# Ten dk stores dealt anew over the DMA engines (nine without engine 4, with strips by SyncE) in the backward pass of decode attention

## The chip, the cores and the metric

One core of one Trainium2 chip. The metric is the device time of one execution in microseconds (us); most executions of one kernel here agree within 0.3%, and differences of a few tenths of a per cent are settled only by several runs of both kernels on the same chip. "Engine 0 to 15" means the 16 DMA engines of the core; PE, DVE, ACT, GpSimd (POOL) and SyncE (SP) are named as such.

## The reference

```python
def _fwd_reference(q, k, v):            # q: (2, 32, 1, 128), k and v: (2, 32, 8192, 128), bfloat16
    scale = q.shape[-1] ** -0.5
    p = softmax(einsum("bhqd,bhkd->bhqk", q, k) * scale)
    return einsum("bhqk,bhkd->bhqd", p, v)

def reference(q, k, v, grad_out):
    out, vjp = jax.vjp(_fwd_reference, q, k, v)
    return out, *vjp(grad_out)          # out, dq, dk, dv
```

One query per head, 64 heads. For each head 2 MB of k and 2 MB of v are read, and 2 MB of dk and 2 MB of dv are written; everything else is small. So the kernel is a stream of 128 loads and 128 stores of 2 MB.

## The kernel before

k and v of a head live in two of twelve tiles of 128 partitions x 64 x 128 bfloat16 (one row of 16 KB per partition). dk and dv are written over k and v in the same tile, the tile is stored, and the load of a head six further on refills it. SyncE issues the loads, GpSimd the stores; each engine issues in program order.

```python
load_eng = nc.sync
store_eng = nc.gpsimd
pin = tc.keep_in_program_order
NTILE = 12
FIRST = 6                       # rows of q loaded by GpSimd at the start: puts its cursor at 6
SPREAD = range(4, 60, 7)        # eight heads whose dk store is split into 126 + 2 rows

def by_rows(eng, dst, src, rows):
    p = 0
    for m in rows:
        pin(eng.dma_start(out=dst[p : p + m], in_=src[p : p + m], max_dma_last_dim=NT * D))
        p += m

def outer(i, w, c, ends):       # writes dv (w = 1) or dk (w = 0) over the tile; at its end:
    ...
        if w == 0 and i in SPREAD:
            by_rows(store_eng, dst, h.tile[w], (P - 2, 2))
        else:
            eng = load_eng if len(ends) > 1 else store_eng     # len(ends) > 1: the last head only
            pin(eng.dma_start(out=dst[:, b0:b1, :], in_=h.tile[w][:, b0:b1, :]))

# in the main loop, O1 and O0 are where dv and dk of a head begin, NCH = 4 steps each
if (i := at(O1 + NCH)) is not None and i + AHEAD < BH:
    load(i + AHEAD, 0)          # refills dv's tile
if (i := at(O0 + NCH)) is not None and i + AHEAD < BH:
    load(i + AHEAD, 1)          # refills dk's tile
if x := within(O1): outer(x[0], 1, x[1], ...)
if x := within(O0): outer(x[0], 0, x[1], ...)
```

## Time and profile before

| what | where it is read | value |
|---|---|---|
| time | 3 runs | 1279.65 us median (1277.72 to 1282.9); the profiled run, slower than all of these, 1285.99 |
| span | first line of the page | 1284.2 us |
| busiest compute engine | part 1 of the page | PE 86% |
| share of the load and store queues | part 3 | 49.9% and 48.8% of 16 engines |
| traffic | part 2 | 539.03 MB; at 428.3 B/ns this is 1258.5 us |

428 GB/s is the rate of every undisturbed stretch. It gives a simple account: span = 1258.5 us + what of the DMA rate is lost before 1200 us + what is lost after 1200 us (the tail: no loads are left then, and the last stores wait for the last compute). The rate itself, in 40 slices of 32 us:

```profile
GB/s 388 427 428 428 428 429 428 427 428 428 428 428 428 420 428 428 428 424 426 428 428 418 425 428 428 422 418 426 428 427 419 422 429 429 426 423 429 428 413 219
```

The slices of 418 to 422 lie at or behind split dk stores. A load takes 19 us from issue to landing, a store over 50 (columns: the transfer, the queue, how often, KB each, median us from issue to landing):

```profile
kvt<-in_v_dram SPq DMA_DIRECT2D x64, 2048.0 KB, 19.1
kvt<-in_k_dram SPq DMA_DIRECT2D x63, 2048.0 KB, 19.4
out_dram<-kvt POOLq DMA_DIRECT2D x8, 2016.0 KB, 55.7
```

### The profile page before, as it was taken

What the parts mean: (1) busy time and instruction counts of PE and PEld (TensorE: products, weight loads), DVE (VectorE), ACT (ScalarE), POOL (GpSimd) and SP (SyncE); (2) the same over time, 40 slices, a digit from 0 to 9 for tenths busy, and PEclk for the clock granted to TensorE, in tenths of its full rate; (3) what the DMA queues carried; (4) which work ended last, traced back from release to release, by engine and by line L of the source; (5) the groups of instructions that cost most, each with busy time, mean ns of one, the idle gap of its engine ahead of it and who ended that gap; (6) DMA issues with size and microseconds to landing.
All of it is one profiled execution on the core that took longest, in us unless ns stands there. A gap on an engine that the chain in (4) does not pass through costs nothing.

```text
span 1284.2 us, 32475 instructions
## 1 busy us (share of the span) xinstructions
PE 1099.4 (86%) x14148; PEld 805.5 (63%) x14148; DVE 1014.6 (79%) x2258; ACT 956.9 (75%) x641; POOL 76.0 (6%) x143
## 2 busy tenths in 40 slices
PE   6899899899889899889899889888888799879870
PEld 5666666666666666666666666666656566656650
DVE  2888888888888888888888888888788688777882
ACT  6777777778778778778778778777778687777750
POOL 0000000000000000000000000000000000000000
PEclk9999999999999999999999999999999899999985
DMA  9999999999999999999999999999999999999995
GB/s 388 427 428 428 428 429 428 427 428 428 428 428 428 420 428 428 428 424 426 428 428 418 425 428 428 422 418 426 428 427 419 422 429 429 426 423 429 428 413 219
DMA packets 40155, 539.03 MB, mean 420 GB/s; under 512 B 5196, under 2 KB 5196, under 8 KB 6476
## 3 DMA queue, kind: packets, MB, share of 16 engines
q1 hardware_dynamic: 20172, 272.70, 49.9%
q0 software_dynamic: 19840, 264.25, 48.8%
q8 instruction: 110, 1.80, 0.5%
q14 instruction: 33, 0.27, 0.1%
HBM read 268.47 MB, written 268.47 MB: 418 GB/s over the span
## 4 chain that ended last, share of the span: by engine, by line
DVE 32%; DMA 17%; issue 14%; another core or an unknown queue 14%; PE 12%; ACT 8%; POOL 1%; SPq 0%; ACTq 0%; POOLq 0%; DVEq 0%
DVE kvt L427 18%; DMA kvt<-in_v_dram 11%; ACT ev L196 8%; PE tp L194 7%; DMA out_dram<-kvt 6%; DVE sel L395 4%; DVE rows L221 3%; DVE sel L389 1%; PE acc L372 1%; DVE pair L303 1%; PE raw L208 1%; ACT E_f L271 1%; DVE dSu L349 1%; PE sw L178 1%
## 5 line engine op out<-in xcount | busy, mean ns | idle before, releaser
L196 ACT COPY ev<-tp 128x2048 bf16<-128x2048 bf16 x512 | 941.3, 1868 | 285.7 <-PE tp L194 280.6
L427 DVE TENSOR_TENSOR kvt<-qb,pair 128x2048 bf16<-128x2048 bf16 x512 | 616.9, 1216 | 0.1
L194 PEld LDWEIGHTS <-kvt 128*128 128x128 bf16 x8192 | 507.0, 102 | 160.7 <-issue 114.4
L194 PE MATMUL tp<-ident_bf,kvt 128*128 128x128 bf16 x8192 | 572.9, 226 | 38.0 <-DMA kvt<-in_v_dram 28.8
L208 PE MATMUL raw<-ev,qdT 128*32 128x512 bf16 x2048 | 210.0, 399 | 5.0 <-ACT ev L196 1.6
L395 DVE SCALAR_TENSOR_TENSOR sel<-acc,diag,sel 128x128 f32<-128x128 f32 x384 | 134.7, 351 | 13.6
L228 PEld LDWEIGHTS sw<-sel,rows 128*128 128x128 f32 x1024 | 124.8, 192 | 29.7 <-issue 12.9
L228 PE MATMUL sw<-sel,rows 128*128 128x16 f32 x1024 | 137.2, 266 | 0.6 <-DVE rl L324 0.6
L372 PE MATMUL acc<-kvt,E_pad 128*32 128x512 bf16 x1024 | 102.9, 391 | 30.6 <-DVE E_pad L280 30.6
L445 POOL DMA_DIRECT2D out_dram<-kvt x118 | 63.3, 536 | 1081.9 <-DVE kvt L427 518.1
L372 PE MATMUL acc<-kvt,dS_pad 128*32 128x512 bf16 x1024 | 111.1, 426 | 0.8 <-DVE dS_pad L358 0.8
L221 DVE COPY rows<-raw 128x512 f32<-128x512 f32 x128 | 87.5, 684 | 26.1 <-PE raw L208 26.1
L178 PE MATMUL sw<-ident_bf,qdT 128*128 128x128 bf16 x128 | 28.5, 223 | 70.9 <-DVE mp L240 70.8
L280 DVE CAST E_pad<-E_f 128x64 bf16<-128x64 f32 x64 | 12.5, 195 | 92.9 <-ACT E_f L271 92.9
L208 PEld LDWEIGHTS <-qdT 128*32 128x32 bf16 x2048 | 64.6, 95 | 25.0 <-issue 18.4
L315 PEld LDWEIGHTS sw<-ld,ones 128*128 128x128 f32 x256 | 38.2, 188 | 54.5 <-issue 29.3
L372 PEld LDWEIGHTS <-E_pad 128*32 128x32 bf16 x1024 | 26.3, 93 | 55.2 <-DVE E_pad L280 40.1
L246 DVE TENSOR_REDUCE gm<-sw 1x1 f32<-1x128 f32 x64 | 17.9, 279 | 49.3 <-PE sw L244 49.3
L409 PE MATMUL acc<-ones,sel 128*128 128x1 f32 x256 | 47.5, 255 | 6.2 <-DVE sel L395 6.2
L315 PE MATMUL sw<-ld,ones 128*128 128x1 f32 x256 | 49.1, 261 | 0.1
L409 PEld LDWEIGHTS acc<-ones,sel 128*128 128x128 f32 x256 | 44.0, 215 | 7.3 <-DVE sel L395 7.3
L389 DVE TENSOR_SCALAR sel<-acc,diag 128x128 f32<-128x128 f32 x128 | 43.8, 342 | 0.0
(49 smaller groups left out, 367.5 us busy)
## 6 DMA issues: line engine op xcount, KB each, us to landing
out_dram<-kvt POOLq DMA_DIRECT2D x118, 2048.0 KB, 51.5
kvt<-in_v_dram SPq DMA_DIRECT2D x64, 2048.0 KB, 19.1
kvt<-in_k_dram SPq DMA_DIRECT2D x63, 2048.0 KB, 19.4
out_dram<-kvt POOLq DMA_DIRECT2D x8, 2016.0 KB, 55.7
out_dram<-kvt SPq DMA_DIRECT2D x8, 512.0 KB, 23.2
kvt<-in_k_dram SPq DMA_DIRECT2D x2, 512.0 KB, 4.5
kvt<-in_k_dram SPq DMA_DIRECT2D x1, 1024.0 KB, 7.2
out_dram<-kvt POOLq DMA_DIRECT2D x8, 32.0 KB, 55.2
```

Source lines behind the costliest of these rows:

```text
L194: pin(nc.tensor.transpose(tp[:, t, :], src[:, c * CH + t, :], ident_bf[:]))
L196: pin(nc.scalar.copy(out=ev[:], in_=tp[:]))
L208: nc.tensor.matmul(h.raw[g * SW : (g + 1) * SW, :], lhsT=qdT[:, w, q0 : q0 + SW], rhs=ev[:, g * QT : (g + 1) * QT, :].rearrange("p n d -> ...
L221: pin(nc.vector.tensor_copy(out=h.rows[:], in_=h.raw[:]))
L228: nc.tensor.matmul(h.score[w].rearrange("p (n t) -> p n t", t=QT)[:, :, t], lhsT=h.rows[:, t * P : (t + 1) * P], rhs=sel4[:].rearrange("p ...
L315: nc.tensor.matmul(out, lhsT=ones[:].to_broadcast([P, P]), rhs=col, start=True, stop=True)
L372: nc.tensor.matmul(h.acc[w][g : g + CW, :], lhsT=wts[:, n0 : n0 + CW], rhs=rows[:, n0 : n0 + QT, :].rearrange("p n d -> p (n d)"), start=( ...
L389: nc.vector.tensor_scalar(out=h.sel[:], in0=block, scalar1=diag[:, 0:1], scalar2=None, op0=ALU.mult)
L395: nc.vector.scalar_tensor_tensor(out=h.sel[:], in0=block, scalar=diag[:, b : b + 1], in1=h.sel[:], op0=ALU.mult, op1=ALU.add,)
L409: nc.tensor.matmul(h.acc[w][:, 0:1], lhsT=h.sel[:], rhs=ones[:], start=True, stop=True)
L427: nc.vector.tensor_tensor(out=h.tile[w][:, n0 : n0 + CH, :].rearrange("p n (e t) -> p n e t", t=2), in0=h.qb[w][:] .rearrange("p (e t) -> ...
L445: pin(eng.dma_start(out=dst[:, b0:b1, :], in_=h.tile[w][:, b0:b1, :]))
```

## The change

Intent: the 16 DMA engines don't end together, so move rows from the late ones to the early ones. Nine dk stores (ONE) leave out engine 4 and one (TWO, head 58) is meant to leave out 7 and 8; the rows left over are dealt with strips, part of them issued by SyncE.

```diff
-FIRST = 6
-SPREAD = range(4, 60, 7)
+FIRST = 5
+ONE = range(4, 58, 6)
+TWO = (58,)
...
-            if w == 0 and i in SPREAD:
-                by_rows(store_eng, dst, h.tile[w], (P - 2, 2))
+            if w == 0 and i in ONE:
+                part(store_eng, dst, h.tile[w], 0, P - 8)             # 120 rows
+                part(store_eng, dst, h.tile[w], P - 8, 5, 0, 4)       # 5 rows, 4 tiles (1 KB)
+                if i == ONE[-1]:
+                    part(load_eng, dst, h.tile[w], P - 3, 3, 0, 4)
+                else:
+                    for n in range(4):
+                        part(store_eng, dst, h.tile[w], P - 3, 3, n, 1)   # 3 rows, 256 B
+                part(load_eng, dst, h.tile[w], P - 8, 7, 4, NT - 4)   # 7 rows by SyncE
+                part(load_eng, dst, h.tile[w], P - 1, 1, 4, NT - 4)   # 1 row by SyncE
+            elif w == 0 and i in TWO:
+                part(store_eng, dst, h.tile[w], 0, P - 16)
+                part(store_eng, dst, h.tile[w], P - 16, 2)
+                part(load_eng, dst, h.tile[w], P - 14, 7)
+                part(load_eng, dst, h.tile[w], P - 7, 7)
```

`part(eng, dst, src, p, rows, n, tiles)` is one DMA of `rows` rows from row p and `tiles` tiles from tile n.

## The prediction

> **What bounds the kernel now.** I read the page from the top. Part 1 shows no engine full: PE is busy 86%, and the chain of waits is split over so many lines that none could carry the end. Part 2 is what matters: the DMA row stays at nine from the first slice to the last but one. Then the list of DMA traffic:
>
> ```profile
> DMA  9999999999999999999999999999999999999995
> ...
> DMA packets 40155, 539.03 MB, mean 420 GB/s; under 512 B 5196, under 2 KB 5196, under 8 KB 6476
> ...
> q1 hardware_dynamic: 20172, 272.70, 49.9%
> q0 software_dynamic: 19840, 264.25, 48.8%
> q8 instruction: 110, 1.80, 0.5%
> ```
>
> q1 is SyncE (the loads), q0 GpSimd (the stores), q8 instruction fetches. 49.9 + 48.8 + 0.6% is a full house: the kernel is bound by DMA. A row of 16 KB takes 611 ns in the packets of the trace; 32,768 rows (128 loads and 128 stores of 128) on 16 engines are 2048 each, 1251 us of the span of 1284. So some 33 us at most are not bulk transfer. Where they are, the view of busy time by stretches says (columns: stretch, us, busy us of PE, PEld, DVE, ACT, POOL, clock, DMA share, GB/s):
>
> ```profile
> 440.00:680.00 240.00, 216.03 (x2786) 158.49 (x2789) 197.95 (x440) 186.72 (x127) 15.07 (x27) 0.95 1.01 427
> 680.00:720.00 40.00, 36.15 (x476) 26.50 (x468) 33.45 (x78) 31.69 (x22) 2.12 (x4) 0.96 1.01 419
> ...
> 1240.00:1262.00 22.00, 11.19 (x83) 6.45 (x82) 18.68 (x40) 3.34 (x4) 0.53 (x1) 0.62 0.94 395
> 1262.00:1284.00 22.00, 0.00 (x0) 0.00 (x0) 0.01 (x1) 0.00 (x0) 0.00 (x0) 0.50 0.33 136
> ```
>
> In the last 22 us no compute engine works and a third of the DMA engines' time is used. The work left at 1240 us is 22 x 0.94 + 22 x 0.33 = 28 us per engine; dealt out evenly it would end at 1268. So the uneven shares of the 16 DMA engines cost 16 us, 1.2%, and that is all this change can go for. The waits of SyncE's own queue show why the slowest engine, not the mean, sets the pace before the end too:
>
> ```profile
> SPq L100 <- DMA out_dram<-kvt: 1138.7, 116, 25.0
> ```
>
> A load needs a tile free, and a tile is free when the last engine has landed its share of the store: SyncE does little but wait for that.
>
> **Which engine is late.** The trace names no DMA engine, but its packets give them back: on one engine the next packet starts 3 or 4 ns before the last one's end, and the order of sizes on each queue is known from the program. I linked the packets from 12.7 to 1250 us into 16 such strings; every packet found a place. Fourteen engines hold 9 rows of each of the eight split dk stores and have no pause at all (eleven) or 2 to 6 us of it; two hold one row of each. The last dk store's 16 completions are the ends: five engines by 1261 us (these had run dry), 1264.3, 1264.8, 1266.3, eight at 1271.1 to 1275.1, and one at 1281.1. The instruction fetches of q8 go round eight of the engines in a fixed order, 13 or 14 each, and one costs its engine about 1.2 us (the fetch takes 0.88 to 1.1 us and the row behind it 1.0 us in place of 0.61), so 14 to 19 us: these eight are the later ones, but for one that has been relieved. The latest and the second latest are four places apart in that round. Of the two relieved engines, A has no fetches, but half of its rows are 20 to 50 ns too slow, all along: 42 us over its 1951 rows, far above the 2 to 15 us of the others. B has fetches, and rows of 611 ns apart from stalls; the relief of 8 x 8 rows (39 us) left it 11 us of pauses: B did not need it.
>
> **What the Trainium skill says.** All four places are in "DMA: Bandwidth & Descriptors".
> - "Why a DMA increments its semaphore by 16 and not by 1": a DMA is dealt to the largest k up to 16 that divides its slowest dimension, on SyncE's path to the lowest-numbered k engines, on GpSimd's to k in a row from a cursor. The trace agrees for GpSimd: 126 rows must go as 9 rows on 14 engines with the cursor at 6 (behind FIRST = 6), leaving out 4 and 5, which then take the 2 rows. In the strings an unused engine gets a 4-byte packet for each packet of the others; then there must be 141 x 16 + 2 = 2258 of SyncE's, 118 x 16 + 16 + 8 x 96 = 2672 of GpSimd's, 256 rows of 256 B and 10 of 8 B, 5196 in all, which is the page's count under 512 B. So A and B are engines 4 and 5.
> - The same section lists an exception with rows rounded up to sixteenths; this kernel's 126 rows do not follow it.
> - "Queues, rings and completion order": an engine takes its queues in turn, a packet each. The strings agree: q0, q1, q0, q1.
> - "Latency and other measured facts": engines 7 and 15 are usually slower. If the fetches go round the odd engines, the two latest are four places apart as 7 and 15 are, and B is 5, A is 4. I take that: latest is 7 (1281.1), next 15 (1275.1).
>
> **The change part by part.** Rows of dk beyond the eight of an even deal, summed over the kernel:
> - Before: eight split stores, +1 for fourteen engines and -7 for 4 and 5: +8 and -56.
> - After, nine stores of ONE: 120 rows go to k = 15 engines from cursor 5, 8 each, none on engine 4. The cursor comes to 4; 5 short rows (1 KB) bring it to 9, four times 3 pieces of 256 B back to 5, so it repeats. Seven rows by SyncE go to engines 0 to 6, one row (k = 1) to engine 0. Over nine: engine 0 +18; 1, 2, 3, 5, 6 +9; 4 -63; 7 to 15 nothing.
> - After, head 58, cursor 9: as the title has it, 112 rows go without 7 and 8 (k = 14), these get one row each of the two, and 14 rows go to 0 to 6: +2 for 0 to 6, -7 for 7 and 8. By the divisor rule 112 would be 7 rows on all 16; then 7 gets -1.
>
> Difference at 611 ns a row: engine 7 -15 rows, -9.2 us; 8 the same; 9 to 15 -8 rows, -4.9; 1, 2, 3, 6 +3 rows, +1.8; 0 +12 rows, +7.3; 4 -5 rows, -3; 5 +67 rows, +41. New ends: 7 at 1281.1 - 9.2 = 1272; 15 at 1275.1 - 4.9 = 1270; 1 and 3 (fetch engines, 1273) at 1275; 5 now has the same rows and fetches as 1 and 3, so 1275 too, its 41 us eating its pauses and its early end. Engine 0 has no fetches; most such ended at or before 1266, so 1273 or less. The end moves from 1281 to 1275: 6 us. The timed median of 1279.65 becomes 1273.5.
>
> GpSimd issues four more DMAs per ONE head at about 0.55 us (the split stores' issues take 0.58 to 0.79), 2 us on an engine that is 6% busy; SyncE two more at 0.35 to 0.5 us: hidden. A single row of 59 for q on engine 0 at the start is 30 more packets of 15 to 22 ns: nothing.
>
> **Rivals.**
> - A new wait: SyncE issues in program order, so the strips of dk stand behind a load that waits for dv's store, and then behind that load's packets (19 us to landing). dk's tile becomes free some 10 us later than now, nine times, and the next load with it. For: the waits line above. Against: q0 has some 50 us of stores queued (51.5 us from issue to landing on the page), so the engines go on. But after the split stores q1 runs dry already (the 419 GB/s at 680 us), and some engines then take 1.2 us for a row of q0; engine strings show 9 to 13 us lost so. If the longer run of small packets doubles this, the gain is eaten: 1280.
> - A and B changed round, so the slow engine is 5: it would get 67 rows of 0.63 us, 42 us more, with 3 us of pauses: about 1300. The redesign relieving 4 alone speaks against it.
> - Engine 0 is one of the later even ones (1271): 1278 profiled, so 1276 timed.
> - All level: 16 us less, 1264. No row of the sum gets there.
>
> **Range and chances.** 1273.5, mostly between 1267 and 1281. Faster by 2% is below 1254, more than the whole unevenness: 1%. Slower by 2%, over 1305, needs the second rival and more: 2%. Within 2%: 97%.
>
> **What would show it.** The stretch after the last compute should be about 6 us shorter with a DMA share over 0.33; the last store's completions should have no single straggler 6 us behind. In the strings one engine should lack all ONE rows and be slow, and the two latest should be fetch engines. The wait of SyncE for stores should have some longer entries at ONE heads. I am wrong if the last engine is 5 or 0 far behind the rest, or if dips below 420 GB/s deepen at the split stores.

## The result, and the profile after

1287.88 us median of 4 runs (1287.23 to 1291.4) against 1280.49 (1277.72 to 1282.9, 4 runs) of the kernel before beside it: ratio 1.0064, 95% interval 1.0036 to 1.0092. Predicted were 1273.5, between 1267 and 1281. So within 2% as predicted, but 7.4 us slower and not 6 us faster. (A ratio here is the mean time of one kernel's fast runs over that of the other's of the same rounds, so not quite the ratio of the medians quoted.) Executions over 1.5% slower than the fastest of the same kernel are left out of the means.

The rate by slices, and the traffic, from the page after:

```profile
GB/s 389 428 428 425 430 424 428 428 423 427 429 428 424 429 427 426 417 427 429 406 421 428 423 426 426 428 421 406 427 428 425 406 428 427 424 424 428 427 422 261
DMA packets 41357, 539.03 MB, mean 419 GB/s; under 512 B 6100, under 2 KB 6151, under 8 KB 7557
```

Not a byte more is moved, but four slices ahead of the tail fall to 417 and 406; the lowest there was 418 before, the first slice apart. The two long stretches of the kernel before, then those of the kernel after (columns as in the prediction's table):

```profile
440.00:840.00 400.00, 360.80 (x4641) 264.35 (x4640) 330.63 (x736) 312.67 (x210) 25.00 (x45) 0.95 1.01 426
840.00:1240.00 400.00, 338.56 (x4452) 248.63 (x4449) 319.94 (x706) 300.95 (x202) 23.05 (x42) 0.97 1.01 426
```

```profile
440.00:840.00 400.00, 360.13 (x4614) 263.44 (x4613) 328.99 (x730) 310.77 (x210) 32.47 (x58) 0.94 1.01 424
840.00:1240.00 400.00, 342.18 (x4420) 249.85 (x4420) 316.51 (x701) 299.89 (x201) 27.74 (x50) 0.94 1.00 422
1240.00:1262.00 22.00, 15.03 (x133) 9.67 (x132) 17.98 (x41) 7.55 (x6) 1.06 (x2) 0.70 0.99 420
1262.00:1284.00 22.00, 2.74 (x14) 1.35 (x14) 6.45 (x12) 0.00 (x0) 0.00 (x0) 0.50 0.52 211
```

2 and 4 GB/s less of 427 over 400 us are 2 + 4 = 6 us of transfer, and they are left for the end: the last 22 us move 211 GB/s where before they moved 136, and PE still works in them. By the account: 1258.5 + 13.7 + 13.0 = 1285.2. The loss sits before 1200 us: 4.7 us more than before there, 3.7 less behind it.

What SyncE does there, in order of time (start, us, queue and line, transfer, how many):

```profile
121.46 0.33 SPq L99 DMA_DIRECT2D kvt<-in_v_dram  x1
131.02 0.33 SPq L99 DMA_DIRECT2D kvt<-in_k_dram  x1
131.44 0.67 SPq L89 DMA_DIRECT2D out_dram<-kvt  x2
167.26 0.37 SPq L99 DMA_DIRECT2D kvt<-in_v_dram  x1
167.74 1.28 SPq L99 DMA_DIRECT2D kvt<-in_k_dram  x1
```

dk of this head was complete at 123 us (GpSimd issued its part at 123.71), but SyncE first had to issue the load ahead, which waited for its tile until 131.02. The two strips then stand behind that load in SyncE's queue: its semaphore records have the load landing at 165.34 and the strips at 166.32 and 167.11, while GpSimd's parts had landed by 150.6. Only then is dk's tile free and the next load issued, 36 us after the last. Before, loads follow each other every 9.8 us here, with gaps of 14 to 17 us at the eight split stores; after, the nine gaps are 36, 31, 24, 18, 18, 19, 18, 19 and 24 us. This is rival 1 of the prediction, and larger than the 10 us it gave. It looked like the whole answer; the experiments say it is not.

### The profile page after: what moved, and what is told of

The parts are those of the page before. It is cut to its first block, busy times and chain, and to the rows that moved or that the text cites.

```text
span 1285.2 us, 32584 instructions
## 1 busy us (share of the span) xinstructions
PE 1108.4 (86%) x14148; PEld 810.2 (63%) x14148; DVE 1014.4 (79%) x2258; ACT 957.4 (74%) x641; POOL 95.3 (7%) x177
## 4 chain that ended last, share of the span: by engine, by line
DVE 44%; DMA 23%; PE 14%; ACT 12%; issue 4%; another core or an unknown queue 1%; SPq 0%; DVEq 0%; ACTq 0%; POOL 0%; POOLq 0%
DVE kvt L426 25%; ACT ev L195 10%; DMA out_dram<-kvt 10%; DMA kvt<-in_v_dram 9%; PE tp L193 9%; DVE sel L394 6%; DVE rows L220 4%; DMA kvt<-in_k_dram 3%; DVE sel L388 2%; DVE pair L302 2%; PE acc L371 2%; PE raw L207 1%; ACT E_f L270 1%; DVE dSu L348 1%
## 5 line engine op out<-in xcount | busy, mean ns | idle before, releaser
L457 POOL DMA_DIRECT2D out_dram<-kvt x116 | 62.4, 538 | 949.7 <-DVE kvt L426 398.4
L89 POOL DMA_DIRECT2D out_dram<-kvt x52 | 31.0, 600 | 206.9 <-DVE kvt L426 107.5
```

Source lines behind the costliest of these rows:

```text
L89: pin(eng.dma_start(out=dst[r], in_=src[r], max_dma_last_dim=tiles * D))
```

## The experiments

Eighteen runs followed, most of five rounds (e5 is one look; e17 and e18 have more); e5 and e18 repeat the kernel before and the changed one. Each is given against the kernel before on the same chip, as ratio with its 95% interval. The rounds ran on different chips, so kernels of different rounds are compared by their ratios and not by their times.

**First round: which part of the change costs?** e1 takes the four short GpSimd pieces out of the changed kernel (a reset of GpSimd's cursor takes their place, the last three rows go by SyncE). e2 and e3 add one suspect each to the kernel before: short pieces by GpSimd, and a strip of one tile of all 128 rows by SyncE. e4 splits ten heads in place of eight, and the two more leave out engines 5 and 6.

```diff
 # e1, in the changed kernel
-                    for n in range(4):
-                        part(store_eng, dst, h.tile[w], P - 3, 3, n, 1)
+                part(load_eng, dst, h.tile[w], P - 3, 3, 0, 4)
 # e2, in the kernel before, at its eight split stores
-                by_rows(store_eng, dst, h.tile[w], (P - 2, 2))
+                part(store_eng, dst, h.tile[w], 0, P - 2, 0, NT - 4)
+                part(store_eng, dst, h.tile[w], P - 2, 2, 0, NT - 4)
+                for n in range(NT - 4, NT):
+                    part(store_eng, dst, h.tile[w], 0, P, n, 1)
 # e3, in the kernel before, at nine heads range(2, 60, 7)
+                pin(store_eng.dma_start(out=dst[:, : NT - 1, :], in_=h.tile[w][:, : NT - 1, :]))
+                pin(load_eng.dma_start(out=dst[:, NT - 1 :, :], in_=h.tile[w][:, NT - 1 :, :]))
 # e4, in the kernel before: ten split heads, the cursor moved to 7 before the last two
-SPREAD = range(4, 60, 7)
+SPREAD = range(4, 60, 6)
```

> The changed kernel with the four 256-byte pieces of each ONE head on GpSimd's queue replaced by a reset of the DMA cursor ahead of the one remaining small piece, and the last three rows sent by SyncE; the deal of rows over the DMA engines stays as in the changed kernel. Theory 1 (GpSimd may have only eight DMAs out, one a semaphore, and the small pieces take these places, so the next whole stores are issued 10 to 30 us late and the engines run out of stores): the loss goes away, ratio to the kernel before 0.998 to 1.002, and GpSimd issues whole stores every 8 to 12 us behind ONE heads too. Theory 2 (the strips on SyncE's queue land behind a load and hold the next load): still 1.005 to 1.008. Theory 3 (the deal of rows alone, which does not relieve the latest engine): still 1.004 to 1.008.

Measured 1288.16 us, 1.0049 (1.0022 to 1.0077). The loss stays without the short pieces. SyncE's load gaps are 42 to 58 us here, against 18 to 36 in the changed kernel, and the loss is no larger.

> The kernel before, with four tiles (columns) of each of its eight split dk stores sent as four small stores of 128 rows of 256 bytes by GpSimd, so six DMAs a head in place of two, and an even deal of the small ones over all engines. Theory 1: slower, ratio 1.004 to 1.010, with gaps of 20 to 30 us between whole stores behind the split heads. Theories 2 and 3: 0.999 to 1.002.

Measured 1280.01 us, 0.9984 (0.9960 to 1.0007). Short pieces by GpSimd cost no time.

> The kernel before, with one tile (256 bytes of each of the 128 rows) of eight or nine otherwise plain dk stores sent by SyncE in place of GpSimd: an even deal, one DMA more on SyncE. Theory 2: the load that waits for this tile is issued 10 to 20 us later than the 10 us beat, ratio 1.004 to 1.008. Theories 1 and 3: the loads are late here too, but the engines have stores enough, 0.999 to 1.002.

Measured 1287.42 us, 1.0045 (1.0019 to 1.0071). A strip by SyncE brings the loss to the kernel before. Its SyncE, at the first of the nine:

```profile
91.05 0.33 SPq L101 DMA_DIRECT2D kvt<-in_k_dram  x1
91.47 0.42 SPq L446 DMA_DIRECT2D out_dram<-kvt  x1
138.18 0.33 SPq L101 DMA_DIRECT2D kvt<-in_v_dram  x1
```

47 us from the strip to the next load.

> The kernel before with ten split dk stores: eight leave out engines 4 and 5 as now, two more leave out 5 and 6. Theory 3 in the form that the strings of the changed kernel give (the latest engine is 6): the latest falls from 1281 to 1272.5 and the next, 12, ends at 1276, 5 us earlier, ratio 0.995 to 0.998. If the latest is 7, as the prediction had it, all but three engines get two rows more: 1.000 to 1.002.

Measured 1281.96 us, 1.0009 (0.9980 to 1.0039): a changed deal of the rows moves nothing that these runs can tell. By what was expected, this is the outcome for a latest engine 7 and not for 6; e5 will show why it decides neither.

**Second round: whose queue?** e5 is the kernel before once more, for a second trace. e6 gives the strips to ACT's queue, e7 gives them to GpSimd with the same share for each engine within a row or so.

```diff
 # e6, in the changed kernel
-                part(load_eng, dst, h.tile[w], P - 8, 7, 4, NT - 4)
-                part(load_eng, dst, h.tile[w], P - 1, 1, 4, NT - 4)
+                part(nc.scalar, dst, h.tile[w], P - 8, 7, 4, NT - 4)
+                part(nc.scalar, dst, h.tile[w], P - 1, 1, 4, NT - 4)
 # e7, in the changed kernel (reset() puts GpSimd's cursor to 0; head 58 likewise)
+                reset()
+                part(store_eng, dst, h.tile[w], P - 8, 7, 4, NT - 4)
+                reset()
+                part(store_eng, dst, h.tile[w], P - 1, 1, 4, NT - 4)
```

> The kernel before once more, for a second trace, as its profiled execution was one of its slower ones. If the latest engine (the one 5 to 6 us behind all others in the last store) is a property of the deal, the last store's completions again end near 1281 us with one straggler and the execution takes 1285 us; if it was chance, the last completions lie within 2 to 3 us of the next and the execution takes 1278 to 1282.

Measured 1281.07 us (one look, span 1279.3). The last store's latest completion is at 1277.5 us, the one before it at 1275.2: no engine alone 6 us behind, as there was in the first trace (1281.1 against 1275.1).

> The changed kernel with every strip that SyncE sends sent by ScalarE's queue instead, nothing else changed. Theory 2a (a strip lands late because it stands behind whole loads in SyncE's ring on each DMA engine, and the load that needs the tile waits for it): on a ring of its own a strip lands within 2 to 5 us of its issue, and the load gaps behind ONE heads shrink from 18 to 36 us to 10 to 18; ratio to the kernel before 0.997 to 1.002. Theory 2b (any strip sent apart, or the deal of rows, costs the time): still 1.004 to 1.008.

Measured 1304.41 us, 1.0176 (1.0150 to 1.0201). The strips landed in 8 to 10 us and the load gaps shrank to 15 to 20 us, as hoped, but ACT paid for it (its queue, then ACT itself, with the idle time in brackets):

```profile
698.09 9.13 ACTq L89 DMA_DIRECT2D out_dram<-kvt  x2
707.31 3.63 ACT L195 COPY ev<-tp 128x2048 bf16<-128x2048 bf16 x2 [10.62 <-DMA kvt<-in_k_dram]
```

The second strip's issue was held until a load had landed, and with it the copies that PE waits for. So this run cannot say what the place in the queue costs.

> The changed kernel with all strips sent by GpSimd, the cursor reset where needed so that the same engines get the same rows to within one row (engines 0 to 6 the seven rows, engine 0 the single one); five DMAs a ONE head. Theory 2 (strips on SyncE): the loss is gone, 0.996 to 1.001, load gaps under 20 us. Theory 3 (the deal of rows): 1.004 to 1.008 as in the changed kernel.

Measured 1281.93 us, 1.0012 (0.9990 to 1.0035). The loss is gone, as far as an interval of this width can say. Its two long stretches run as before the change:

```profile
440.00:840.00 400.00, 360.73 (x4641) 264.19 (x4640) 330.73 (x735) 312.95 (x211) 31.77 (x56) 0.95 1.01 427
840.00:1240.00 400.00, 348.51 (x4478) 254.67 (x4474) 321.43 (x711) 303.99 (x205) 29.69 (x53) 0.95 1.01 426
```

Two things follow: the loss lies in SyncE carrying the strips, and the new deal itself gains nothing that shows. The load gaps are still 16 to 20 us at these heads.

**Third round: is it the hold of the tile?** e8 leaves the stores of the kernel before alone and adds, where e3 had its strip, a SyncE DMA of 128 short pieces that nobody waits for. e9 moves the load ahead behind the strips; e10 does that in the kernel before.

```diff
 # e8, in the kernel before, at e3's nine heads
+                pin(load_eng.dma_start(out=spare[:], in_=k_v[i][:, NT - 1 :, : D // 2]))
 # e9 in the changed kernel, e10 in the kernel before
-        if (i := at(O1 + NCH)) is not None and i + AHEAD < BH:
-            load(i + AHEAD, 0)
         if (i := at(O0 + NCH)) is not None and i + AHEAD < BH:
+            load(i + AHEAD, 0)
             load(i + AHEAD, 1)
```

> The kernel before, its stores untouched; at the same nine heads and the same place in SyncE's order as in e3_strip_in_before, SyncE gets one more DMA of 128 short pieces, but it reads k into a spare buffer that nobody waits for, so no tile of dk is held by it. If the loss comes because dk's tile is released only when the strip has landed, behind a whole load: no loss, 1280 us, ratio within 0.998 to 1.002, and load gaps of about 10 us at these heads (sum of the excess about 50 us as in before). If it comes because small packets stand among the loads in SyncE's rings, or from SyncE's extra issues: ratio 1.003 to 1.006 as e3.

Measured 1289.12 us, 1.0051 (1.0033 to 1.0070). No tile is held, loads stay nearly as regular as before (what the gaps over 12 us exceed 9.8 us by, summed from 40 to 1200 us, is 53 us; 46 to 48 before), and the loss is as large as e3's.

> The changed kernel, with the load that refills dv's tile moved behind dk's store in program order, so that SyncE issues the strips at once when dk's last part is written (about 123 us in place of 131 us in the first of them) and ahead of that load and not behind it. By the theory that the strip stands behind that load, most of the loss goes: strips land 8 to 15 us earlier, load gaps at the nine heads fall from 18-36 us towards 10-20 us, and the time is 1280 to 1283.5 us, ratio 1.000 to 1.003. If the loss is from the strips as such or from the loads ahead of the earlier one (the one issued at 121 us and still moving), it stays at 1286 to 1289, ratio 1.005 to 1.007.

Measured 1291.81 us, 1.0077 (1.0056 to 1.0098). The strips do go out earlier and ahead of the load:

```profile
121.01 0.33 SPq L99 DMA_DIRECT2D kvt<-in_v_dram  x1
122.17 0.65 SPq L89 DMA_DIRECT2D out_dram<-kvt  x2
131.13 0.37 SPq L99 DMA_DIRECT2D kvt<-in_k_dram  x1
157.71 0.36 SPq L99 DMA_DIRECT2D kvt<-in_v_dram  x1
```

The same sum of excess gaps falls from 121 us in the changed kernel to 75, and the kernel gets no faster.

> The control of e9_load_after_strip: the kernel before with the same move of the load and nothing else. The loads wait for dv's store, which lands later than dk is written, so the moved load should be issued when it was: 1280 us, ratio 0.998 to 1.002. If it is slower, the cost of the move has to be taken from e9's.

Measured 1279.70 us, 0.9981 (0.9963 to 1.0000): the move costs nothing by itself. My theory, the hold of dk's tile, had fallen on both sides.

**Fourth round: turns, hold, rows.** The packets of e8 show something else: in the trace, the packet that follows a 128 B packet on its engine is one of the store queue in 1025 of the 1082 places where it can be told (436 rows of 16 KB, 438 half rows of the split stores, 151 packets of 4 B); 45 times it is another 128 B packet. Each short packet of SyncE thus lets a packet of the stores pass, at most a 16 KB row, so 8 of them on an engine put the loads up to 8 x 0.61 = 4.9 us back (an estimate from the 611 ns of a row); the packets of e8's first strip start between 131.4 and 137.5 us.

```diff
 # e11: e8 with 16 pieces        out=spare[:16], in_=k_v[i][:16, NT - 1 :, : D // 2]
 # e13: e8 with 256 pieces       two DMAs of 128 pieces of 64 B
 # e12: e3, with 112 of the 128 pieces by GpSimd
-                pin(load_eng.dma_start(out=dst[:, NT - 1 :, :], in_=h.tile[w][:, NT - 1 :, :]))
+                pin(store_eng.dma_start(out=dst[: P - 16, NT - 1 :, :], in_=h.tile[w][: P - 16, NT - 1 :, :]))
+                pin(load_eng.dma_start(out=dst[P - 16 :, NT - 1 :, :], in_=h.tile[w][P - 16 :, NT - 1 :, :]))
 # e14: in the kernel before, at e3's heads: 112 rows by GpSimd, 16 whole rows by SyncE
+                pin(store_eng.dma_start(out=dst[: P - 16], in_=h.tile[w][: P - 16]))
+                pin(load_eng.dma_start(out=dst[P - 16 :], in_=h.tile[w][P - 16 :]))
```

> e8_strip_holds_nothing with 16 short pieces in place of 128, so one packet on each engine in place of eight. Theory of turns: each engine takes its queues in turn a packet each, so eight short packets of SyncE let eight 16 KB rows of stores pass and put the loads 8 x 0.61 = 4.9 us back each time; with one packet it is 0.6 us, and the loss is gone: 1280 to 1281.5 us, ratio 0.998 to 1.001. If each extra DMA of SyncE has a fixed cost whatever its size, the loss stays as in e8: ratio 1.004 to 1.006.

Measured 1279.52 us, 0.9976 (0.9953 to 0.9998). A SyncE DMA more has no fixed cost.

> e8_strip_holds_nothing with each strip as two DMAs of 128 pieces of 64 B, so sixteen turns of an engine in place of eight, and nothing held. By the theory of turns the loads are put back 9.8 us each time, and the loss about doubles: ratio 1.008 to 1.012, 1290 to 1296 us. If e8 lost for another reason (a fixed cost of the strip) it stays near 1.005.

Measured 1304.78 us, 1.0176 (1.0140 to 1.0212), more than the double. The loads come late, and the end waits for compute (1240 to 1290 us, second row of the two still full of PE work):

```profile
1240.00:1262.00 22.00, 19.76 (x266) 14.22 (x263) 17.45 (x39) 18.66 (x14) 1.06 (x2) 0.99 0.57 238
1262.00:1290.00 28.00, 20.39 (x232) 13.90 (x228) 24.75 (x58) 13.45 (x10) 1.59 (x3) 0.84 0.67 277
```

So turns are a real cost, and the explanation of e8. They can hardly be the changed kernel's: its strips are two packets on engines 0 to 6 and one more on engine 0, and e11's one packet an engine cost nothing.

> e3_strip_in_before with 112 rows of the strip given to GpSimd, so that SyncE stores the last 16 short pieces alone, one packet on each engine. dk's tile is still held until SyncE's piece has landed behind the whole load ahead of it, as in e3, but only one turn is taken on each engine. If holding the tile costs the time, it stays at e3's ratio of 1.003 to 1.006 with load gaps of 40 to 70 us at these heads; if the turns cost it, 1280 to 1281.5 us, ratio 0.998 to 1.001.

Measured 1284.09 us, 1.0016 (0.9993 to 1.0039), with gaps of 45 to 54 us at these heads. Against e11 on the same chip, which differs by the hold and by 112 short pieces of GpSimd but not by SyncE's turns, these are 4.6 us of medians: with a hold of 50 us goes a cost of some 0.4%.

> The kernel before, whose strip heads give 112 rows of dk to GpSimd (seven on each engine) and 16 whole rows to SyncE (one on each engine): the same row on every engine, so no unevenness between engines and few packets, but dk's tile is held until SyncE's rows have landed behind the load ahead. If the hold costs the time: ratio 1.003 to 1.006 as e3. If the turns of e3, or the uneven shares of SyncE's queue in the changed kernel (two or three packets on engines 0 to 6, none on the others), cost it: ratio 0.998 to 1.002.

The median of the four fast runs is 1298.5 us (1293.02 to 1306.43), the ratio 1.0128 (1.0088 to 1.0168). Even shares, few packets, the hold of e12, and yet the largest loss of a store by SyncE. Here the expectation of both theories is missed.

**Fifth round: the changed kernel taken apart, on the base of e7.** e15 leaves all of dk to GpSimd; e16 gives SyncE the last 256 B piece of each split store (the hold without the packets), e15 adds a copy of 7 rows of k to a scratch area in DRAM (the packets without the hold), e17 has both. e18 is the changed kernel again.

```diff
 # e15: rows by GpSimd on engines 7 to 14, and
+                part(load_eng, scratch, k_v[i], 0, 7, 4, NT - 4)
 # e16
-                part(store_eng, dst, h.tile[w], P - 1, 1, 4, NT - 4)
+                part(store_eng, dst, h.tile[w], P - 1, 1, 4, NT - 5)
+                part(load_eng, dst, h.tile[w], P - 1, 1, NT - 1, 1)
 # e17: e15, and behind the copy
+                part(load_eng, dst, h.tile[w], P - 1, 1, NT - 1, 1)
```

> All of dk is stored by GpSimd as in e7_all_by_gpsimd (engine 4 relieved, the eight rows put on engines 7 to 14), and SyncE gets, at the place of the changed kernel's strips, one DMA of the same form (7 rows of 60 tiles, two packets of 7680 B on each of engines 0 to 6) that copies k to a scratch area in DRAM and holds no tile. It moves 0.97 MB more in all, 2.3 us at 428 GB/s. If the hold of dk's tile is the changed kernel's loss: 1281 to 1285 us, ratio 1.001 to 1.004 (e7's 1.001 and the extra bytes). If SyncE's uneven packets as such are: ratio 1.006 to 1.009.

Measured 1284.46 us, 1.0030 (0.9998 to 1.0062), of which the 0.97 MB more are 0.0018.

> e7_all_by_gpsimd with the very last piece of each of the nine split stores (one tile of one row, 256 B) given to SyncE: dk's tile is held until that piece has landed behind a load, as in the changed kernel, but SyncE's queue has one short packet more on engine 0 and nothing else. If the hold is the changed kernel's loss: 1285 to 1289 us, ratio 1.004 to 1.007, with load gaps of 18 to 36 us at these heads as in the changed kernel. If SyncE's uneven packets are: 1279 to 1283 us, ratio 0.999 to 1.002.

Measured 1282.82 us, 1.0019 (0.9986 to 1.0051), with gaps of 35, 25, 18, 15, 18, 17, 18, 17 and 18 us, nearly those of the changed kernel. The gaps are there, the loss is not seen; but six runs do not rule it out, since the interval reaches 1.0051.

> e15_packets_without_hold and e16_hold_without_packets in one kernel: all of dk by GpSimd but the last 256 B piece of each of the nine split stores, which SyncE stores behind the scratch copy of 7 rows, so the tile is held until both have gone through SyncE's queue. If the changed kernel's loss is the two together and neither alone: ratio 1.006 to 1.010 (1.8 tenths of a per cent of it the extra bytes), DMA time lost around the dry moments of the load ring near the 7.6 us of the changed kernel and not the 3.5 to 3.8 us of e15 and e16, SyncE's load gaps 18 to 38 us. If they only add: ratio about 1.004. If e17 is as good as e7 (1.001 to 1.003), the loss needs dk's own rows in SyncE's queue.

Measured 1286.22 us over 22 runs, 1.0016 (1.0000 to 1.0031). The two together do not make the loss either: 0.0018 of it are the extra bytes, and the changed kernel, in the same rounds, is next.

> The changed kernel once more, as the control of e17 and to see whether its trace repeats: 1286 to 1290 us, ratio 1.004 to 1.008, and 6.5 to 9 us of DMA time lost around the nine dry moments of the load ring, with windows below 410 GB/s at three or more of them.

Measured 1288.21 us over 14 runs, 1.0042 (1.0027 to 1.0057): the loss is there again, and so is the pattern in the trace, as follows.

**Where the time is lost.** I took the bytes moved in each half microsecond between 40 and 1200 us against 428.3 B/ns, and marked the moments where SyncE's queue runs dry (for 1.5 us or more less than one of 16 engines moves a load). What is missing from 12 us ahead of such a moment to 4 us behind it is put down to it. Worked out from the packets of each trace, in us (a second working from the same traces gives all of them within 0.6):

```
kernel                dry moments  lost at them  elsewhere | lost to 1200  after 1200  span
before (3 traces)         5, 6, 6  1.8  2.0 2.0  3.9 1.7 2.5 | 9.0 7.1 7.7  16.7 13.7 14.3  1284.2 1279.3 1280.5*
e11 sixteen pieces              6       1.4         1.4     |     6.2        13.8      1278.5
e7 all by GpSimd                8       3.4         1.4     |     7.9        10.1      1276.5
e16 hold alone                  9       3.8         1.3     |     8.2        14.5      1281.2
e15 packets alone               8       3.5         2.2     |     8.9         9.7      1279.4
changed                         9       7.6         2.9     |    13.7        13.0      1285.2
changed again (e18)             9       7.5         2.6     |    13.4        12.8      1284.7
e9 load after strip             9       9.4         3.9     |    16.5        17.3      1292.3
e3 strip                        8       8.5         4.1     |    15.8        11.7      1286.0
e14 sixteen rows                8       8.8         5.4     |    17.6        15.1      1291.2
e1 changed, no short pieces    10       8.1         3.5     |    15.4        13.2      1287.1
e12 long hold, few packets      8       6.6         2.6     |    12.5        10.5      1281.5
e17 packets and hold            9       6.5         2.6     |    12.3        18.6      1291.7
e8 turns                        3       1.5         6.8     |    11.6        21.3      1291.8
e2 short by GpSimd              7       8.2         1.7     |    13.1         6.5      1278.1
e4 relieve 5 and 6              7       2.5         3.5     |     9.3        11.5      1279.3
e6 strips by ACT                8      11.4         5.7     |    20.6        16.9      1296.0
e13 twice the turns             0       0.0        10.5     |    13.8        28.4      1301.1
* the third is e10
```

Two different losses come apart here. Short packets of SyncE (e8) cost little DMA rate at dry moments; they put the loads behind the stores, and the tail grows to 21 us. Strips of dk by SyncE (the changed kernel twice, e1, e9, e3, e14) cost 7.5 to 9.4 us at the dry moments, where the same deal by GpSimd costs 3.4. For the changed kernel against e7 it is 5.8 us before 1200 us; by the ratios, 1.0064 and again 1.0042 against 1.0012, the two are 4 to 7 us apart. But strips by SyncE are not the only way to such a loss: e2, with all of dk by GpSimd, loses 8.2 us at its dry moments, and e6, with the strips by ACT, 11.4. The table says where the time goes, not that SyncE's queue alone can make it go. One such moment, of the changed kernel and then of e16, with the same gap of 18 us between loads (columns: stretch, us, busy times, clock, DMA share, GB/s):

```profile
636.00:639.00 3.00, 3.00 (x33) 2.29 (x31) 1.57 (x3) 1.61 (x2) 1.59 (x3) 0.70 0.88 357
639.00:645.00 6.00, 5.47 (x78) 4.25 (x78) 4.85 (x12) 4.75 (x6) 0.53 (x1) 1.00 1.02 424
645.00:648.00 3.00, 3.00 (x49) 2.15 (x42) 2.93 (x9) 2.92 (x2) 0.00 (x0) 1.00 1.00 360
```

```profile
632.00:635.00 3.00, 3.00 (x28) 2.08 (x26) 1.23 (x5) 1.87 (x1) 0.53 (x1) 0.52 0.98 412
635.00:639.00 4.00, 3.42 (x49) 2.25 (x47) 2.07 (x4) 3.39 (x4) 0.53 (x1) 1.00 1.01 426
639.00:642.00 3.00, 3.00 (x41) 2.41 (x40) 2.86 (x10) 2.40 (x2) 0.53 (x1) 1.00 1.01 388
```

While the queue of loads is dry the stores alone keep the full rate in these two (424 and 426), so being dry need not cost anything (in e2 it does: 341 GB/s at a DMA share of 0.89 from 993 to 999 us). Time is lost at the two edges. At the second edge, when the next load starts, some of the rows in flight take 0.9 to 1.3 us in place of 0.61: both kernels pay there, 360 and 388 GB/s. At the first edge the changed kernel has a DMA share of 0.88: by that, some engines have neither a load nor a store to move. e16 has 0.98 there. Over all nine moments the first edge costs the changed kernel 7.6 - 3.0 = 4.6 us and e7 1.6; the second edge 3.0 and 1.8. And the moments with the longest holds, the first three (36, 31 and 24 us), cost only 0.3 to 0.4 us each, those at 638, 878 and 999 us 1.4 to 1.8 each: it is not the length of the hold that counts. Nor is a long hold free: e12 and e17 lose 6.6 and 6.5 us at these moments, e16 3.8.

e2 and e12 are a warning: they lose nearly as much at their dry moments, and e2 is no slower and e12 hardly, since their tails are 6.5 and 10.5 us and not 13. Loss of rate before 1200 us and the tail must be read together.

**What stays open.** Why dk's own rows in SyncE's queue leave engines without work, when a copy of equal size with a hold (e17) mostly does not; e17's profiled run was its slowest (1293.49), six of its 22 runs lie around 1281 and most others around 1287, and there is no trace of a faster one. e14, the largest loss by SyncE, is no better explained, and why e2 loses as much at its dry moments with no row in SyncE's queue is open too. Nor did I establish which engines go idle at the first edge: the trace names none, and the linking of packets into engines did not get through these stretches in the later runs.

## Why the prediction was wrong

**The step that failed on the cost side** is the sentence on issues: "SyncE two more at 0.35 to 0.5 us: hidden", together with rival 1's "Against: q0 has some 50 us of stores queued ... so the engines go on." The issue is hidden indeed, and at dry moments the stores do go on at full rate, as rival 1 said. But putting rows of dk into SyncE's queue costs 4 to 7 us (e7 at 1.0012 against the changed kernel at 1.0064 and 1.0042), charged as nothing in the sum. I priced an issue and should have priced a place in a queue. Rival 1 named the wait, with "some 10 us later" for what was 14 to 26 us in the first three heads (gaps of 36, 31 and 24 us for 9.8) and 8 to 14 in the rest, where e7, which holds nothing, has gaps of 16 to 18 us too. But e16 has nearly this wait without the strips and measures 1.0019, not told apart from e7's 1.0012, and e17, with 22 runs, 1.0016 beside the 1.0042 of the changed kernel. What came true is rival 1's last thought, that losses at the dry moments eat the gain: they grew by 4 us against e7 (7.6 for 3.4), and there was no gain for them to eat. By what path the rows in SyncE's queue do this is not shown.

**The step that failed on the gain side** is "I take that: latest is 7 (1281.1), next 15 (1275.1)". Engine names were put to the 16 strings by supposing that instruction fetches go round the odd engines. The changed kernel gives small groups of engines row patterns of their own, so its packets name the engines better: in its trace and in e18's the strings with fetches have either the 1 KB row and SyncE's strips (5 and 6) or the first or the second piece of three rows (9 to 11, 12 to 14). So fetches go round 5, 6 and 9 to 14, and neither 7 nor 15 has any, while both of the latest engines had them. Carried back to the trace before by the order of the round, with B as 5, the latest would be 6 and the second latest 12. This last step is argued, not shown, and e4, which was built on it, did not bear it out (1.0009, where 0.995 to 0.998 was expected). The prediction's own sum gives engine 6 three rows more, and as head 58 was in fact dealt it gets two (nine of ONE and one of head 58 for the eight it had), +1.2 us, not -9.2: with these names the sum says no gain at all. A second error in the same step: the lone engine 6 us behind was a matter of that execution. The trace of e5 has none (1277.5 against 1275.2), and the profiled run before was slower than the timed ones beside it (1285.99 against at most 1282.9). Both e4 and e7 time a new deal at nothing that shows: 1.0009 and 1.0012.

**What held.** The kernel is bound by DMA, before and after. Engine 4 is the slow one of the two relieved, as "A is 4" took it: the string with the slow rows lacks the rows of ONE, and rival 2's 1300 us did not come. The divisor rule held where the title of the change says otherwise: head 58's 112 rows went as seven on each of 16 engines, by GpSimd's 2876 packets of 4 B, where a deal over 14 engines would leave 32 more. So engines 7 and 8 were never relieved by it. GpSimd's short pieces were as free as the prediction had them, though not for its reason: GpSimd did wait for them, on the DMA eight issues earlier (at 593.58 and 603.25 us for instance), which e1 and e2 show to be harmless.

**By its own signs.** "I am wrong if ... dips below 420 GB/s deepen at the split stores": they did, from 418 to 406, and that is where the loss shows. The DMA share of the last stretch rose from 0.33 to 0.52, the sign named for the gain, but because work had been left over for it: a sign that can come from either side is no sign. No engine ended alone 6 us behind (the last store's latest completions are at 1283.8 and 1280.7 us), as hoped, but with no gain; and SyncE's longest wait for a store grew only from 25.0 to 26.5 us.

**Chances.** The class of within 2% was right. The range of 1267 to 1281 allowed the lost gain and no cost; the unknown names of the engines should have put half of the chances above 1280.

## What to carry to other kernels

In a stream bound by DMA the queue that issues a transfer is part of its cost, even where issuing is free: a few rows of a store put into the queue of the loads cost 0.4 to 1.3% here, and the same deal with all rows in the queue of the stores cost nothing that five rounds could tell (0.9990 to 1.0035). Why, the runs do not show, and single short pieces (e12, e16) cost too little to be told. Short packets cost a turn each, so give them to the queue that is ahead (e2), never to the one that is behind (e8, e13). And before moving rows between engines, take a second trace of the same kernel: the late engine of one execution may not be late in the next.

## What the Trainium skill lacked or had wrong

All points are on "DMA: Bandwidth & Descriptors".

- "Queues, rings and completion order" has an engine drain a packet of about 9 to 17 descriptors from a ring before it switches. Here it switched after each packet of the profile (no run shows whether that is the page's packet or its descriptor): a store packet followed a 128 B packet of SyncE in 1025 of 1082 cases, and sixteen short packets an engine in place of eight moved the ratio from 1.0051 to 1.0176. What this does to a queue of short packets is not said.
- "Issuing engines are not separate DMA queues" says that issuing from several engines saves only issue time. It lacks the other side: the same rows issued by SyncE gave a ratio of 1.0064 (1.0042 when repeated), by GpSimd 1.0012.
- "Latency and other measured facts" calls engines 7 and 15 usually slower. Here it was engine 4 whose rows took 20 to 50 ns longer, half of them, and the later engines were those with instruction fetches, 5, 6 and 9 to 14, at about 1.2 us a fetch. I found no page that says that these fetches load eight of the 16.
- "Why a DMA increments its semaphore by 16 and not by 1" lists an exception for some copies of GpSimd, with rows rounded up to sixteenths, and does not say for which. 126 rows did not follow it here: their packets are 9 on each of 14 engines, as the plain divisor rule has it.
- I found no page that has what a queue running dry costs: nothing while it is dry in two kernels (424 and 426 of 428 GB/s; but 341 in e2), and 360 to 388 GB/s over the 3 us in which it starts again, with some rows of 0.9 to 1.3 us for 0.61.
